# An attention and long-convolution kernel: the prologue's seed stages three slots sooner, first maxima over eight PSUM tiles, second unit's leading maxima ahead of the loop

## The chip, the cores and the metric

The kernel runs on one core of a Trainium2 chip. The time is that of one execution on the device, in microseconds (us); below it all durations come from one profiled execution. Engines are named as in the profile: PE (TensorE, matmuls; PEld its weight loads), DVE (VectorE), ACT (ScalarE), POOL (GpSimd), and SP (SyncE), which here issues the DMAs. Each engine executes its instructions in the order in which they stand, and an instruction that waits holds up what stands behind it on its engine.

## The reference

Two independent results are laid side by side in the output. Part A is a state-space convolution over 2048 positions and 448 channels; part B is softmax attention over 2048 positions with 16 heads of 28.

```python
def _A_ref(u, log_A_real, A_imag, C_real, C_imag, log_dt, D_skip):
    dt = jnp.exp(log_dt)
    A = -jnp.exp(log_A_real) + 1j * A_imag
    C = (C_real + 1j * C_imag) * dt[:, None]
    P = jnp.exp((A * dt[:, None])[:, :, None] * pos[None, None, :])
    K = 2.0 * jnp.einsum("dn,dnl->dl", C, P).real
    ...
    return y + u * D_skip[None, None, :]

def _B_ref(x, wqkv, wo):
    ...
    scores = jnp.einsum("bhqd,bhkd->bhqk", q, k) * scale
    p = _softmax(scores, axis=-1)
    o = jnp.einsum("bhqk,bhkd->bhqd", p, v)
    return (lambda x, *d: x.transpose(*d))(o, 0, 2, 1, 3).reshape(B, S, D) @ wo

a = _A_ref(A_u, A_log_A_real, A_A_imag, A_C_real, A_C_imag, A_log_dt, A_D_skip)
b = _B_ref(B_x, B_wqkv, B_wo)
return jnp.concatenate([a, b], axis=-1)
```

y is the causal convolution of u with K, done with FFTs. All data are float32; the kernel keeps precision by splitting operands in a high and a low part (xh and xl, hl).

## The kernel before, in words

**Two phases.** `body` has a prologue and a loop. The prologue projects x to q, k and v (part B) and computes the seeds of the powers of exp(A dt) (part A). It keeps both in DRAM. The loop runs 16 units (4 groups of 4 heads by 4 chunks of 512 queries) by 16 key tiles. In each step it computes scores (`s_mm`, tile pss), their exponentials on ACT (p), the products with v (`pv_step`, tile po), one part of the row maxima of the next unit (`max_mm`), and pieces of part A.

**The prologue's projections.** x comes in four chunks of 512 rows (`load_x`, tile xn). Each chunk is transposed on PE into pt tiles, split into xh and xl, and multiplied with the weights (wqkv, loaded into tri tiles, split by ACT and DVE into khat, vh and vl). There are 12 jobs a chunk, 48 in all: 8 of q or k and 4 of v, each 12 matmuls into one of three PSUM tiles pm (`w_tile`). ACT and DVE then evacuate it into hl (or xn in the last chunk) or vst, and SP writes it out. For k of the first two chunks, ACT and DVE form kb too, and POOL its low part dhl. The place of khat is that of the weights at first: head j of group 0 is loaded there (`load_k`) when both projections of group j in the last chunk are done.

**The seeds.** There are eight seeds (`seeds(o)`), each a list of stages: load the parameters (nat), exponentials and products with dt on ACT, transposes into a pn tile, phases and sizes, range reduction on DVE, sines on ACT, bases on POOL, complex products on DVE (px, pn, sg) and POOL (qhat, x_e), and two writes (sd). Parameters of the first one are loaded by `load_nat(0)`; dt is an exponential built from small DVE instructions on sg tiles (`exact_exp`), turned by PE in `turn_dt`.

**What sets the order.** Stages go into slots: stage i of seed o into slot 4 o + i, the loads two slots ahead of the seed (line 540). Before each slot's stages, as many projections are issued as PW = 37 slots need for 48 jobs. So there were 41 slots, the last four of them seeds alone. Within the prologue a scheduler then moves instructions on each engine; from `nc.kept = KEPT["a"]` (line 903) on, program order is kept. Each DMA carries one of eight completion names in rotation (DMAHW0 to DMAHW7), and waits for the earlier DMA that carried the same one.

**Unit 0's maxima** (lines 576 to 589). For each of 16 row blocks i, two pairs are reduced: kc 0 and 1 (`max_mm`, with kdif) and kc 2 and 3 (`max_pair`, with q_neg, the negated queries, so that PE forms a difference). Of each pair, ACT writes the Relu of the first tile into rl; DVE adds it to the second tile and takes the maximum (`tensor_tensor_reduce`, the CUSTOM_DVE_ANT rows). These use five PSUM tiles in turn, two pt and three pm, and two rl buffers. `max_join` and `max_end` turn the maxima (mh), and `max_put` writes them as two rows of unit 0's qhat, which the loop's first score matmul reads. Then the first LEAD = 3 blocks of unit 1's maxima follow, with four matmuls each.

Of the kernel before, what the change touches and what calls it, by code (L numbers as in the profile page):

```python
# [18 lines left out]
D = 448  # L19

H = 16
# [17 lines left out]
S0, SP, SW, SD, PW, E3 = 0, 4, 0, 5, 37, 8  # L39
# [51 lines left out]
def body(ctx, tc, a, out):  # L91
# [81 lines left out]
    def max_pair(i, kc, ps, q_neg):  # L173
        j, t = divmod(i, 4)
        ts = slice(t * 128, (t + 1) * 128)
        pm, kt = ps(), kt_g[0][j]
        if kc == 2:
            nc.tensor.matmul(pm, q_u[0][:, j, ts], kt[:, 2 * CQ:3 * CQ], start=True, stop=False)
            nc.tensor.matmul(pm, q_neg[:, j, ts], kt[:, 3 * CQ:], start=False, stop=True)
            rl_u[0, i] = kd_p.tile([128, CQ], F32, name="rl", bufs=2)  # L180
            nc.scalar.activation(rl_u[0, i], pm, AF.Relu)
        else:
            nc.tensor.matmul(pm, q_u[0][:, j, ts], kt[:, 3 * CQ:], start=True, stop=True)
            rl = rl_u.pop((0, i))
            nc.vector.tensor_tensor_reduce(rl, pm, rl, 1.0, -3.0e38, ALU.add, ALU.max, m_u[0][:, j, t, 1:2])
# [40 lines left out]
    with ExitStack() as st:  # L226
# [18 lines left out]
        load_x(0)  # L245
        w_g = k0_t[:CK].rearrange("p g (i s k h e) -> p i s k g h e", i=2, s=2, k=NCK, h=HG)
        vh = y_p.tile([CK, NCK, D], F32R, name="vh")
        vl = y_p.tile([CK, NCK, D], F32R, name="vl")
        nc.gpsimd.memset(k0_t[:CK].rearrange("p g (n e) -> p (g n) e", e=32)[:, :, DH:].bitcast(F32), 0.0)
        vst = [x_p.tile([128, H, 32], F32, name=f"vst{i}") for i in range(2)]  # L250
        for t in vst:
            nc.gpsimd.memset(t[:, :, DH:DH + 1], 1.0)
            nc.gpsimd.memset(t[:, :, DH + 1:], 0.0)
        wns = []
        for i in range(2):
            wn = t_p.tile([128, 3, LV, BO * 16], F32, name="tri", bufs=2).rearrange("p t k h -> p (t k h)")
            wn = wn[:CK, :2 * 3 * D].rearrange("p (k s d) -> p k s d", k=2, s=3)
            wns += [wn[:, 0], wn[:, 1]]
        for k in range(NCK):
            nc.sync.dma_start(wns[k], wqkv[k * CK:(k + 1) * CK, :].rearrange("p (s d) -> p s d", s=3))  # L260
        nc.sync.dma_start(kones, a["kones"])

# [3 lines left out]
        def load_nat(o):  # L266
            nats[o] = s_p.tile([PO, 4, 256], F32, name="nat", bufs=2)
            for i, n in enumerate(("A_log_A_real", "A_A_imag", "A_C_real", "A_C_imag")):
                nc.sync.dma_start(nats[o][:, i, :], bass.AP(tensor=a[n].tensor, offset=a[n].offset + first(o) * 256,
                                                            ap=[[256, JF // 4], [JF * 256, 4], [1, 256]]))  # L270
# [6 lines left out]
        for f in range(2):  # L277
            nc.sync.dma_start(ldt[4 * f:4 * f + 4, :].rearrange("o (j i) -> o j i", j=4), bass.AP(
                tensor=t.tensor, offset=t.offset + f * DF, ap=[[JF // 4, 4], [JF, 4], [1, JF // 4]]))
        load_nat(0)  # L280
        pw2 = s_p.tile([128, LV], F32, name="pw2")
        nc.sync.dma_start(pw2, a["pw2"])
        half_pi = s_p.tile([128, 1], F32, name="half_pi")
        nc.gpsimd.memset(half_pi, TWO_PI / 4)
        nc.sync.dma_start(sel, a["sel"])
        nc.sync.dma_start(w1, a["w1"])
        for k in range(NCK):
            for s in (1, 0):
                src = wns[k][:, s, :].rearrange("p (g h e) -> p g h e", g=G, e=DH)
                hi, lo = (w_g[:, i, s, k, :, :, :DH] for i in range(2))  # L290
                nc.scalar.activation(hi, src, AF.Copy)
                nc.vector.tensor_tensor(lo, src, hi.bitcast(F32), ALU.subtract)
            nc.scalar.activation(vh[:, k, :], wns[k][:, 2, :], AF.Copy)
            nc.gpsimd.tensor_tensor(vl[:, k, :], wns[k][:, 2, :], vh[:, k, :].bitcast(F32), ALU.subtract)
# [25 lines left out]
        def turn_dt():  # L320
            dt_ps = ps_t.tile([128, CQ], F32, name="pt")[:PO, :NO]
            nc.tensor.transpose(dt_ps, dt_o, ident[:NO, :NO])
            for i, f in enumerate((1.0, 0.15915494309189535, 2.0, -2.0, -1.0)):
                nc.vector.tensor_scalar(dt_all[:, i, :], dt_ps, f, None, op0=ALU.mult)

# [208 lines left out]
        n_stage = SP * (NO - 1) + len(stages[0])  # L534
# [3 lines left out]
        for o in range(NO):  # L538
            for i, st_ in enumerate(stages[o]):
                slots[max(SP * o + (i or -2), 0)] += st_  # L540
        slots[1].insert(0, turn_dt)
# [34 lines left out]
        more = [lambda: ps_t.tile([128, CQ], F32, name="pt")] * 2 + [w_tile] * 3  # L576
        n_st = ExitStack()
        q_neg = pool(n_st, "n_p").tile([128, HG, CQ], F32R, name="q_neg")
        for j in range(HG):
            nc.scalar.activation(q_neg[:, j], q_u[0][:, j].bitcast(F32), AF.Copy, scale=-1.0)  # L580
        for i in range(16):
            for kc in range(4):
                f, kw = (max_mm, (0, i, kc)) if kc < 2 else (max_pair, (i, kc))
                f(*kw, more[(4 * i + kc) % 5], *([q_neg] if kc > 1 else []))
        nc.scalar.activation(half_pi[:1], half_pi[:1], AF.Exp)
        n_st.close()
        max_join(0, 2)
        max_end(0, ps_t.tile([128, CQ], F32, name="pt"))
        max_put(0, nc.scalar)
# [314 lines left out]
    for b in range(3):  # L904
        load_sd(b, nc.sync if b else nc.scalar)
    for i in range(LEAD):
        for kc in range(4):
            max_mm(1, i, kc)
# [260 lines left out]
```

## Time and profile before

| what | value |
|---|---|
| median of 3 runs | 1283.33 us (1280.13 to 1284.64) |
| the profiled execution | 1284.67 us |
| its span, first to last instruction | 1282.8 us |
| mean granted PE clock | 0.981 |
| busy share of the span: PE, DVE, ACT, POOL | 95%, 72%, 75%, 66% |
| first score matmul of the loop | 234.41 us |

Line numbers hardly help in this profile: nearly every instruction passes through one helper (line 75), so rows are told apart by the names of the tiles that they write and read (out<-in). In a row of the timeline stand the start, the duration, the engine, the tiles and, in brackets, how long the engine had been idle and what released it. In a row of groups stand the busy time, the mean duration in ns and the idle time ahead. In the table by stretches each engine's busy time stands with its number of instructions, then the granted clock, the busy share of the DMA engines and the rate. The page's 40 slices show where the kernel is not full: PE dips in the sixth and seventh, that is from about 160 to 224 us.

```profile
PE   7988867999999999999999999999999999999987
POOL 2466651798778888877689999989995222324321
PEclk9988888899999999999999999999999999999999
```

### The profile page before, as it was taken

The numbers are of one execution on the slowest core, as the hardware profiler recorded it, in microseconds if no ns is written. First come the engines' busy times: TensorE is split into PE (matmuls) and PEld (weight loads), VectorE is DVE, ScalarE is ACT, GpSimd is POOL, SyncE is SP. The second block draws the span as 40 slices with busy tenths as digits, with TensorE's granted clock in tenths as the row PEclk, the third lists the DMA queues.
The fourth block names the chain that finished last, engine by engine and source line by source line (L and its number), as shares of the span: only waits on it lengthen the run. The fifth ranks groups of instructions, "written<-read, shape, count | busy, mean of one in ns | idle before, by whom it ended". The sixth has DMA issues, their size and how long they took to land.

```text
span 1282.8 us, 33335 instructions
## 1 busy us (share of the span) xinstructions
PE 1223.7 (95%) x12641; PEld 700.9 (55%) x12641; DVE 925.5 (72%) x2106; ACT 967.8 (75%) x2162; POOL 843.4 (66%) x728
## 2 busy tenths in 40 slices
PE   7988867999999999999999999999999999999987
PEld 5867754455555555555555555555555555544433
DVE  5788877787877787878778888888887645645111
ACT  4978856688888888888888888888887666656452
POOL 2466651798778888877689999989995222324321
PEclk9988888899999999999999999999999999999999
DMA  6767887446664544465533223432324533657665
GB/s 210 263 242 241 265 301 290 127 93 182 172 154 106 156 133 146 128 214 195 169 102 91 61 76 106 149 88 71 83 59 154 175 135 132 205 171 227 194 171 165
DMA packets 200089, 205.36 MB, mean 160 GB/s; under 512 B 95992, under 2 KB 158520, under 8 KB 197880
## 3 DMA queue, kind: packets, MB, share of 16 engines
q1 hardware_dynamic: 199720, 202.87, 51.4%
q8 instruction: 100, 1.64, 0.5%
q10 hardware_dynamic: 208, 0.36, 0.1%
q14 instruction: 61, 0.50, 0.1%
HBM read 120.73 MB, written 82.18 MB: 158 GB/s over the span
## 4 chain that ended last, share of the span: by engine, by line
PE 77%; DVE 7%; ACT 5%; POOL 5%; issue 3%; DMA 2%; SPq 0%; ACTq 0%; POOLq 0%; DVEq 0%
PE pm L75 44%; PE pss L75 16%; PE po L75 16%; POOL e L75 1%; ACT tri L75 1%; DVE mx L75 1%; ACT rl L75 1%; PE pt L75 1%; POOL qhat L75 1%; DVE sg L75 1%; DVE hl L75 1%; DVE tri L75 1%; POOL x_e L75 1%; DVE px L75 1%; POOL p L75 1%
## 5 line engine op out<-in xcount | busy, mean ns | idle before, releaser
L75 ACT ACTIVATE p<-pss 128x512 f32<-128x512 f32 x1024 | 561.4, 611 | 112.8 <-PE pss L75 108.5
L75 PE MATMUL pss<-qhat,khat 128*128 128x512 f32 x1024 | 402.7, 399 | 1.5 <-ACT p L75 1.4
L75 DVE TENSOR_REDUCE mx<-pm 128x1 f32<-128x512 f32 x480 | 308.6, 684 | 109.6 <-PE pm L75 107.5
L75 PE MATMUL pm<-khat,qhat 128*128 128x512 f32 x749 | 326.4, 439 | 5.3 <-ACT rl L75 3.0
L75 POOL TENSOR_TENSOR e<-e,sdb 128x256 f32<-128x256 f32 x168 | 201.9, 1202 | 108.1 <-ACT e L75 62.4
L75 PE MATMUL po<-p,v 128*32 128x512 f32 x2048 | 269.1, 594 | 0.0
L75 POOL TENSOR_TENSOR e<-e,eu 128x256 f32<-128x256 f32 x168 | 248.0, 1476 | 13.2
L75 PEld LDWEIGHTS pm<-khat,qhat 128*128 128x128 f32 x749 | 141.4, 189 | 201.3 <-ACT p L75 52.0
L75 DVE CUSTOM_DVE_ANT_0 rl<-pm,rl 128x512 f32<-128x512 f32 x259 | 178.4, 689 | 71.6 <-ACT rl L75 68.4
L75 PEld LDWEIGHTS pss<-qhat,khat 128*128 128x128 f32 x1024 | 190.4, 188 | 46.1 <-issue 10.8
L75 POOL TENSOR_TENSOR eu<-e,sdb 128x256 f32<-128x256 f32 x168 | 202.0, 1202 | 0.0
L75 POOL TENSOR_TENSOR p<-pr,pr 64x448 f32<-64x448 f32 x64 | 73.1, 1142 | 160.4 <-PE pm L75 135.2
L75 ACT ACTIVATE rl<-pm 128x512 f32<-128x512 f32 x259 | 157.1, 607 | 12.7 <-PE pm L75 7.9
L75 DVE TENSOR_TENSOR g<-g,zg 128x128 f32<-128x128 f32 x392 | 162.2, 414 | 3.4
L75 PE MATMUL pm<-kdif,qhat 128*128 128x512 f32 x249 | 101.1, 406 | 8.5 <-DVE xn L75 6.6
L75 PE MATMUL pm<-xh,khat 112*128 112x512 f32 x256 | 87.0, 422 | 9.2 <-DVE kb L75 4.4
L75 DVE TENSOR_TENSOR zg<-g,zg 128x128 f32<-128x128 f32 x224 | 87.9, 393 | 5.1
L75 PEld LDWEIGHTS pm<-e,g 128*32 128x32 f32 x3584 | 57.2, 109 | 43.8 <-issue 16.1
L75 DVE TENSOR_TENSOR pr<-pm,ub 128x448 f32<-128x448 f32 x64 | 37.0, 620 | 56.2 <-PE pm L75 41.8
L75 PE MATMUL pm<-e,g 128*32 128x64 f32 x3584 | 73.0, 222 | 1.9 <-POOL e L75 1.9
L75 ACT ACTIVATE y<-pm 128x448 f32<-128x448 f32 x48 | 26.5, 553 | 58.2 <-PE pm L75 34.1
L75 ACT ACTIVATE ub<-pm 128x224 f32<-128x224 f32 (+1 forms) x96 | 38.8, 450 | 39.9 <-PE pm L75 37.6
(134 smaller groups left out, 1465.5 us busy)
## 6 DMA issues: line engine op xcount, KB each, us to landing
sdb<-sd SPq DMA_DIRECT2D x55, 336.0 KB
qhat<-q SPq DMA_DIRECT2D x64, 256.0 KB
khat<-k SPq DMA_DIRECT2D x64, 256.0 KB
sd<-sg SPq DMA_DIRECT2D x8, 1456.0 KB
k<-hl SPq DMA_DIRECT2D x16, 512.0 KB
mw<-in_mw SPq DMA_DIRECT2D x16, 512.0 KB
sd<-qhat SPq DMA_DIRECT2D x8, 896.0 KB
yu_d<-ub SPq DMA_DIRECT2D x64, 112.0 KB
```

Source lines behind the costliest of these rows:

```text
L75: i = f(*args, **kw)
```

## The change

Five things are done.

1. `SH = 3` takes three slots off every stage; the load, too, from slot 4 o - 2 to 4 o - 5 (none below slot 0). The number of slots falls from 41 to 38 (the projections still use 37). `turn_dt` moves from slot 1 to slot 0.
2. The parameters come first: dt's loads, `load_nat(0)` and dt's exponential move ahead of the loads of x and the weights, and their six DMAs go on ACT's queue in place of SP's. kones is loaded after pw2.
3. Unit 0's maxima take eight PSUM tiles in turn (two pt, two pn, one px, three pm) in place of five, and in the order kc 0, 2, 1, 3. The rl of the second pair comes from a pool of its own with three buffers, so there are five in all.
4. The three leading blocks of unit 1 are computed in the prologue, over the same eight tiles, right behind `max_put`. Their PSUM tiles belong to the prologue's pools, whose places the loop's tiles take later.
5. `max_put(0)` and the first sd load go on SP's queue, where they had been on ACT's.

```diff
-S0, SP, SW, SD, PW, E3 = 0, 4, 0, 5, 37, 8
+SP, SH, PW, E3 = 4, 3, 37, 8
...
-    def max_pair(i, kc, ps, q_neg):
+    def max_pair(i, kc, ps, q_neg, rl_p):
...
-            rl_u[0, i] = kd_p.tile([128, CQ], F32, name="rl", bufs=2)
-            nc.scalar.activation(rl_u[0, i], pm, AF.Relu)
+            rl_u[0, i, 1] = rl_p.tile([128, CQ], F32, name="rl", bufs=3)
+            nc.scalar.activation(rl_u[0, i, 1], pm, AF.Relu)
...
+        def load_nat(o, queue=nc.sync):
+            nats[o] = s_p.tile([PO, 4, 256], F32, name="nat", bufs=2)
+            for i, n in enumerate(("A_log_A_real", "A_A_imag", "A_C_real", "A_C_imag")):
+                queue.dma_start(nats[o][:, i, :], bass.AP(tensor=a[n].tensor, offset=a[n].offset + first(o) * 256,
+                                                          ap=[[256, JF // 4], [JF * 256, 4], [1, 256]]))
...
+            nc.scalar.dma_start(ldt[4 * f:4 * f + 4, :].rearrange("o (j i) -> o j i", j=4), bass.AP(
+                tensor=t.tensor, offset=t.offset + f * DF, ap=[[JF // 4, 4], [JF, 4], [1, JF // 4]]))
+        load_nat(0, nc.scalar)
...
         load_x(0)
...
-        n_stage = SP * (NO - 1) + len(stages[0])
+        n_stage = SP * (NO - 1) + len(stages[0]) - SH
...
-                slots[max(SP * o + (i or -2), 0)] += st_
-        slots[1].insert(0, turn_dt)
+                slots[max(SP * o + (i - SH if i else -2 - SH), 0)] += st_
+        slots[0].insert(1, turn_dt)
...
-        more = [lambda: ps_t.tile([128, CQ], F32, name="pt")] * 2 + [w_tile] * 3
+        p_t, p_n, p_x = (lambda p=p, n=n: p.tile([128, CQ], F32, name=n) for p, n in ((ps_t, "pt"), (ps_n, "pn"), (ps_x, "px")))
+        more = [p_t, w_tile, p_t, w_tile, p_n, w_tile, p_n, p_x]
...
         for i in range(16):
-            for kc in range(4):
-                f, kw = (max_mm, (0, i, kc)) if kc < 2 else (max_pair, (i, kc))
-                f(*kw, more[(4 * i + kc) % 5], *([q_neg] if kc > 1 else []))
+            for n, kc in enumerate((0, 2, 1, 3)):
+                ps = more[(4 * i + n) % 8]
+                max_mm(0, i, kc, ps) if kc < 2 else max_pair(i, kc, ps, q_neg, n_p)
         nc.scalar.activation(half_pi[:1], half_pi[:1], AF.Exp)
-        n_st.close()
         max_join(0, 2)
-        max_end(0, ps_t.tile([128, CQ], F32, name="pt"))
-        max_put(0, nc.scalar)
+        max_end(0, p_t())
+        max_put(0, nc.sync)
+        for i in range(LEAD):
+            for kc in range(4):
+                max_mm(1, i, kc, more[(4 * i + kc + 1) % 8])
+        n_st.close()
         sst.close()
...
     for b in range(3):
-        load_sd(b, nc.sync if b else nc.scalar)
-    for i in range(LEAD):
-        for kc in range(4):
-            max_mm(1, i, kc)
+        load_sd(b)
```

The scheduler makes a new order of the whole prologue from this. Three places show it. The first is the start on SP, with the completion names that each DMA waits for. Before:

```order
L75 DMA ident<-in_ident 128x128
L75 DMA xn<-in_B_x 128x2x448 x2
L75 DMA tri<-in_B_wqkv 112x1344 x4
L75 DMA kones<-in_kones 128x1
L75 DMA sg<-in_A_log_dt 4x4x14 [waits DMAHW0_49]
L75 DMA sg<-in_A_log_dt 4x4x14 [waits DMAHW1_49]
L75 DMA nat<-in_A_log_A_real 56x1x256 [waits DMAHW2_49]
```

Now, on SP:

```order
L75 DMA ident<-in_ident 128x128
L75 DMA xn<-in_B_x 128x2x448 x2
L75 DMA tri<-in_B_wqkv 112x1344 [waits DMAHW1_49]
L75 DMA tri<-in_B_wqkv 112x1344 [waits DMAHW2_49]
L75 DMA tri<-in_B_wqkv 112x1344 [waits DMAHW3_49]
L75 DMA tri<-in_B_wqkv 112x1344 [waits DMAHW4_49]
```

and on ACT, at its very start, where no DMA stood before:

```order
L75 DMA sg<-in_A_log_dt 4x4x14 x2
L75 DMA nat<-in_A_log_A_real 56x1x256
L75 DMA nat<-in_A_A_imag 56x1x256
L75 DMA nat<-in_A_C_real 56x1x256
L75 DMA nat<-in_A_C_imag 56x1x256 [waits DMAHW0_49]
L75 ACT_TABLE_LOAD
L75 ACTIVATE nat<-nat 56x256 [waits DMAHW4_49]
L75 ACTIVATE xh<-pt 112x512 [waits PE_49] x2
```

Five of the parameters' six DMAs are now among the first eight, which need not wait for a name; the weight loads (tri) no longer are. And ACT's first xh stands behind six issues and the first exponential.

The second place is DVE where the last seed ends. `xn<-pm_..., xn` is the evacuation of the last projection; px, sg and qhat rows are seeds; rows with `rl,mx` are unit 0's maxima. Before:

```order
L75 TENSOR_TENSOR sg<-sg,px 128x2x7x16
L75 TENSOR_TENSOR xn<-pm_1939,xn 128x512
L75 TENSOR_TENSOR qhat<-qhat 128x7x16
L75 TENSOR_TENSOR px<-qhat 128x112
L75 TENSOR_TENSOR qhat<-qhat 128x7x16
L75 TENSOR_TENSOR qhat<-qhat,px 128x7x16
L75 TENSOR_TENSOR px<-qhat 128x112
L75 TENSOR_TENSOR qhat<-qhat,px 128x7x16
L75 TENSOR_TENSOR px<-pn,gz 128x224
L75 TENSOR_TENSOR sg<-pn,tri 128x2x7x16
L75 TENSOR_TENSOR px<-sg,px 128x224
```

Now:

```order
L75 TENSOR_TENSOR px<-pn,gz 128x224
L75 SCALAR_TENSOR_TENSOR hl<-pm_1954,kones,hl 128x512
L75 TENSOR_TENSOR sg<-sg,px 128x2x7x16
L75 TENSOR_TENSOR sg<-px,tri 128x2x7x16
L75 TENSOR_TENSOR px<-px,gz 128x224
L75 TENSOR_TENSOR sg<-sg,px 128x2x7x16
L75 TENSOR_TENSOR xn<-pm_1987,xn 128x512
L75 ISA rl,mx<-pt,rl 128x512
L75 ISA mx 128x1
L75 ISA rl,mx<-pn,rl 128x512
L75 ISA mx 128x1
```

Before, fourteen seed rows stood between the last evacuation and the first maximum; now none does, and the first maxima alternate between pt and pn tiles.

The third place is ACT between unit 0's last rl, the maxima's transfer (qhat<-mh) and unit 1's leading rl. Before:

```order
L75 ACTIVATE rl<-pm_2261 128x512
L75 ACTIVATE rl<-pt 128x512
L75 ACTIVATE rl<-pm_2276 128x512
L75 DMA qhat<-mh 1x16x128 x2
L75 DMA sdb<-sd_81 128x672
L75 ACTIVATE rl<-pm_2326 128x512
```

Now:

```order
L75 ACTIVATE rl<-pm_2258 128x512
L75 ACTIVATE rl<-pn 128x512
L75 ACTIVATE rl<-pm_2273 128x512
L75 ACTIVATE rl<-pm_2295 128x512
L75 ACTIVATE rl<-pm_2308 128x512
L75 ACTIVATE rl<-pm_2321 128x512
```

The three DMAs have left ACT; they stand on SP behind the last write of sd, with the sdb and ua loads behind them.

72 lines of the change are left out of this document (34 added, 38 removed).

## The prediction

> **What bounds the kernel now.** The profiled execution took 1284.67 us, 1282.8 of them the span; the median of the three runs is 1283.33, 1.34 below it. I read the busy time by stretches first, cut where the chain of waits changes: start-up; the projections with the seeds between them; the seeds' tail; unit 0's maxima; unit 1's leading maxima; the loop.
>
> ```profile
> core 0: us, PE busy (x) PEld busy (x) DVE busy (x) ACT busy (x) POOL busy (x), PEclk, DMA share, GB/s
> 0.00:20.00 20.00, 11.93 (x42) 9.13 (x43) 7.91 (x12) 9.26 (x17) 7.15 (x20) 1.00 0.72 204
> 20.00:143.00 123.00, 109.37 (x506) 87.76 (x504) 101.38 (x206) 100.48 (x247) 70.47 (x92) 0.94 0.74 252
> 143.00:180.20 37.20, 36.69 (x158) 30.08 (x158) 28.22 (x48) 30.73 (x74) 15.46 (x20) 0.92 0.76 253
> 180.20:195.40 15.20, 2.54 (x6) 1.34 (x5) 12.51 (x28) 3.48 (x14) 13.60 (x19) 0.60 1.02 359
> 195.40:224.90 29.50, 25.02 (x75) 14.52 (x75) 21.47 (x64) 20.42 (x37) 1.34 (x2) 0.86 0.75 276
> 224.90:234.40 9.50, 7.10 (x14) 3.64 (x15) 5.88 (x15) 2.30 (x5) 1.08 (x2) 0.64 0.65 208
> 234.40:1282.80 1048.40, 1031.03 (x11843) 554.38 (x11841) 748.14 (x1738) 801.11 (x1771) 734.32 (x577) 1.00 0.47 139
> ```
>
> The loop holds PE for 1031.03 of 1048.40 us and the change touches nothing in it, so I carry its 1048.4 us over whole. What can move is the 234.4 us ahead of it. There PE sits nearly empty in one stretch, 180.2 to 195.4 (2.54 us busy, clock 0.60), while DVE (12.51) and POOL (13.60) finish the last seeds. In the last quarter of the projections, 143 to 180.2, PE is full (36.69 of 37.2); in 20 to 143 no engine is full, DVE and ACT stand at 82%.
>
> The chain of waits, in order of time, shows how the hole and the two stages behind it hang together:
>
> ```profile
> 188.18 0.70 DVE xn L75
> 188.88 0.04 issue
> 188.93 0.50 PE pm L75
> 189.43 5.75 DMA khat<-k
> 195.18 0.39 ACT sg L75
> 195.58 0.43 ACT rl L75
> 196.00 2.07 ACT q_neg L75 x4
> ...
> 225.91 1.90 DMA qhat<-mh
> 227.83 0.61 ACT rl L75
> 228.48 6.10 PE pm L75 x10
> ```
>
> The last projection, whose matmuls ended at 180.2, has its low part formed by DVE only at 188.18, behind seed rows. The last eight khat loads and ACT's copies of the seeds (sg at 195.18) stand before the first rl. So the seeds set the start of unit 0's maxima, through the in-order queues of ACT, DVE and SP.
>
> **The hole (seeds three slots sooner).** The DVE order shows the effect: the last seed's rows now lie ahead of the last projection's evacuation, which the maxima follow at once. Of the 12.51 us of DVE in the hole two evacuations are no seeds (0.73 and about 0.67, rows below), so 11.1 us of DVE work must fit ahead of PE's end. In return the parameters' exponential goes to the start:
>
> ```profile
> L75 DVE TENSOR_TENSOR xl<-pt,xh 112x512 fp32r<-112x512 f32 x4 | 2.8, 692 | 9.6 <-ACT xh L75 9.6
> L75 DVE TENSOR_SCALAR sg<-sg 8x56 f32<-8x56 f32 x10 | 1.7, 174 | 0.2
> L75 DVE TENSOR_TENSOR sg<-sg 8x56 f32<-8x56 f32 x6 | 1.7, 276 | 0.1
> L75 DVE SCALAR_TENSOR_TENSOR hl<-pm,kones,hl 128x512 fp32r<-128x512 f32 x2 | 1.5, 732 | 0.0
> L75 DVE TENSOR_TENSOR hl<-pm,hl 128x512 fp32r<-128x512 f32 x1 | 0.7, 671 | 0.0
> L75 DVE SCALAR_TENSOR_TENSOR sg<-sg 8x56 f32<-8x56 f32 x3 | 0.6, 204 | 0.1
> L75 DVE COPY sg<-sg 8x56 f32<-8x56 f32 x1 | 0.2, 203 | 0.0
> L75 DVE CAST sg<-sg 8x56 int32<-8x56 f32 x1 | 0.2, 171 | 0.0
> ```
>
> These sg rows are 1.7 + 1.7 + 0.6 + 0.2 + 0.2 = 4.4 us, and the 9.6 us that DVE waits before the first xl rows hide them. Net 6.7 us of DVE work is added between 20 and 180.2, where DVE is free for 21.6 + 9.0 = 30.6 us. If that work ran at the 82% of the stretch 20 to 143, the projections would end 6.7 / 0.82 = 8.1 us later; if it all fell into waits, 0. Between the two I take 3: it lands in the first chunks, which no engine fills, and the last 37 us are held by PE anyway, where DVE has 9 us free. PE's end is then 183.2. Behind it stand ACT's evacuation (0.6), the first rl (0.6), and up to 0.5 of seed rows on DVE; the first maximum on DVE starts at about 185. Before, it started at 196.04 (row below). **Gain 11.0, bounds 3 and 14**: 14 if the projections end no later; 3 if they end 8.1 later and the first khat loads cost another 3, about half of the 5.75 above. POOL's 13.6 us moves too; POOL is 57% busy from 20 to 143, so I cost it at nothing beside the 3 us. If that cover fails, evacuations that wait for POOL hold PE; that is the slower rival.
>
> **Parameters first, on ACT's queue.** The order puts six issues ahead of ACT's first work, and SP's four weight loads now each wait for an earlier load; before they went out without a wait.
>
> ```profile
> 2.17 1.95 SPq L75 DMA_DIRECT2D tri<-in_B_wqkv  x4
> 4.63 1.60 SPq L75 DMA_DIRECT2D sg<-in_A_log_dt  x2
> 4.66 2.23 PE L75 MATMUL pt<-ident,xn 128*112 128x128 f32 x8 [4.66 <-DMA xn<-in_B_x]
> 6.28 1.02 SPq L75 DMA_DIRECT2D nat<-in_A_log_A_real  x1
> 9.53 1.04 ACT L75 ACTIVATE khat<-tri 112x448 fp32r<-112x448 f32 x2 [2.44 <-DMA tri<-in_B_wqkv]
> ```
>
> The first x load had landed at 4.66. If the first weight load waits for it, it goes out 2.5 us later than at 2.17; the end on the other side is 0, since DMA engines were 0.72 busy up to 20 us and the x loads come first anyway. ACT's six issues take 1.6 + 4 x 1.0 = 5.6 us by these rows, and ACT had no weights to work on before 9.53, which covers them. **Cost 1.0, bounds 0 and 2.5**, nearer to 0 because the queue is kept busy by x meanwhile. [...]
>
> **Unit 0's maxima over eight tiles.** 32 reductions run on DVE from 196.04 to 224.91, 28.9 us:
>
> ```profile
> L75 DVE CUSTOM_DVE_ANT_0 rl<-pm,rl 128x512 f32<-128x512 f32 x19 | 13.0, 690 | 5.8 <-ACT rl L75 4.4 <-PE pm L75 0.9
> L75 DVE CUSTOM_DVE_ANT_0 rl<-pt,rl 128x512 f32<-128x512 f32 x13 | 9.0, 690 | 2.7 <-ACT rl L75 2.3
> L75 ACT ACTIVATE rl<-pm 128x512 f32<-128x512 f32 x19 | 11.1, 596 | 4.5 <-PE pm L75 3.4 <-DVE mx L75 0.6 <-PE pt L75 0.3
> L75 ACT ACTIVATE q_neg<-qhat 128x512 fp32r<-128x512 f32 x4 | 2.2, 618 | 0.0
> ...
> 196.04 0.69 DVE L75 CUSTOM_DVE_ANT_0 rl<-pt,rl 128x512 f32<-128x512 f32 x1 [1.06 <-ACT rl L75]
> ```
>
> DVE's work stays (21.5 us). Its idle, 5.8 + 2.7 less the 1.06 ahead of the first, is 7.4, nearly all waiting for ACT's rl, which waited for PE, which waited for one of five tiles or two rl buffers. Now there are eight tiles and three more rl buffers for the folded half. ACT's q_neg, 2.2 us in one piece plus an rl of 0.6, still holds DVE once. That leaves about 2.9 us idle. **Gain 4.5, bounds 0 and 7.4.** PE has room: 25.02 us at a mean clock of 0.86, less if the clock is whole.
>
> **Unit 1's leading maxima ahead, one queue.** DVE stands still between the mh rows and the first leading rl, since ACT issues the mh transfers and one sdb load ahead of its rl:
>
> ```profile
> 225.86 0.28 DVE L75 SCALAR_TENSOR_TENSOR mh<-pt,mh 16x128 fp32r<-16x128 f32 x1
> 225.91 1.25 ACTq L75 DMA_DIRECT2D qhat<-mh  x2
> 228.46 0.69 DVE L75 CUSTOM_DVE_ANT_0 rl<-pm,rl 128x512 f32<-128x512 f32 x1 [2.32 <-ACT rl L75]
> 229.08 1.28 DVE L75 TENSOR_REDUCE mx<-pm 128x1 f32<-128x512 f32 x2
> 234.41 0.41 PE L75 MATMUL pss<-qhat,khat 128*128 128x512 f32 x1
> ```
>
> The 2.32 us go, as the transfers move to SP. There qhat<-mh stands behind the last sd write, and sdb and ua loads stand behind it. The mh transfer took 1.90 and the leading reductions take three times 0.69 + 1.28 = 5.9 us, so the transfer is hidden. The loop's score tiles lie where the eight tiles lay and must wait for DVE to read the last of those, which gives part of it back. **Gain 1.5, bounds 0 and 2.3.**
>
> Sum: 11.0 - 1.0 + 4.5 + 1.5 = 16.0. From 1284.67 that is 1268.7, and 1.34 less for the median: **1267 us**.
>
> **Rivals.** (a) The projections pay in full: DVE keeps its 82%, PE ends at 188.3, the hole yields 5.9; the sum is 10.9 and the time 1272. For it: no engine is full and yet PE loses 13.6 us from 20 to 143, so waits are set by in-order queues and not by load. Against: the 9.6 us at the start. (b) The khat loads hold the maxima: the DMA engines are 1.02 busy at 359 GB/s in the hole, and SP issues in order behind the q and k writes. If the load at the chain's 5.75 stays whole behind PE's end, the first maxima start 5 us later: sum 11, again 1272; against it, only the rows of heads 0 and 1 are needed first, and their place is released two projections sooner. (c) Both, with no gain from the tiles because the 690 ns reductions keep waiting for ACT: 16.0 - 5.1 - 5 - 4.5 = 1.4, so 1282. (d) Slower: PE starves in the projections. Seed rows now precede evacuations on ACT and DVE; three projection tiles wait for them, PE idles, and its clock falls as in the hole (0.60). With a mean clock of 0.80 in place of 0.94 over 20 to 143, 109.4 us of matmuls become 128.5, 19 more, and idle added to it 5: PE ends at 204, the first reduction starts at 206, the hole gives -10, the start -1; with 4.5 and 1.5 that is 5 us slower, 1288, and more where it starves longer. The sign turns at a PE end of 199. Against it: the clock held 0.94 at about the same seeds per chunk.
>
> **How the numbers follow.** Forecast 1267: 0.50. (a) 0.18, (b) 0.14, (c) 0.10, (d) 0.08. All bounds at their best give 14 + 7.4 + 2.3 = 23.7 and 1259.6; (c) is near their worst. The range 1258 to 1281 leaves out (d) and half of (c). About 0.3%, 3.85 us, is what a measurement tells from no change: faster means below 1279.5. The forecast, (a), (b) and a little of (c) are faster: 0.84; the rest of (c) and a mild (d) are the same: 0.09; slower 0.07.
>
> **What would show it.** After the change: PE's last projection matmul at about 183 with no stretch of 10 us below 30% busy behind it; the first reduction rl at about 185 (later than 190 speaks for (a) or (b): for (a) if PE's end is late too, for (b) if DVE then waits for a khat load); 32 reductions in about 24 us, idle once for q_neg; ACT's first khat row at about 10.5; less than 1 us of DVE idle between mh and the next rl; the first pss at about 218.4; 1048 us from there. A loop longer than 1050 us, or a PE end past 199, would make the prediction wrong.

## The result and the profile after

The changed kernel takes 1279.87 us (median of 20 runs, 1276.66 to 1282.5) against 1282.09 us of the kernel before (20 runs, 1280.07 to 1284.64): ratio 0.9985, 95% interval 0.9978 to 0.9992. That is 2.2 us less, where the prediction had 16.0 and a time of 1267. The time lies inside the predicted range, near its upper end, but the gain is within the 0.3% that was called no change. The ratio of the repetition (again, below) leaves out two slow executions, of 1364.71 and 4017.98 us.

The profiled execution of the changed kernel took 1278.54 us. The table by stretches, cut at its own stages: start, projections (two rows), from PE's last projection matmul to the first reduction, unit 0's reductions, unit 1's lead, loop.

```profile
core 0: us, PE busy (x) PEld busy (x) DVE busy (x) ACT busy (x) POOL busy (x), PEclk, DMA share, GB/s
0.00:20.00 20.00, 12.51 (x44) 9.13 (x45) 11.22 (x38) 11.05 (x22) 6.97 (x20) 1.00 0.89 239
20.00:143.00 123.00, 109.23 (x487) 86.80 (x486) 100.41 (x186) 100.28 (x252) 74.43 (x97) 0.90 0.70 242
143.00:186.80 43.80, 39.91 (x179) 31.92 (x178) 34.04 (x65) 31.11 (x76) 27.94 (x34) 0.96 0.80 257
186.80:190.80 4.00, 1.54 (x5) 0.98 (x5) 1.46 (x3) 1.97 (x5) 1.72 (x2) 0.90 0.96 360
190.80:220.00 29.20, 24.55 (x76) 16.55 (x75) 20.79 (x64) 18.81 (x34) 0.00 (x0) 0.78 0.97 347
220.00:228.20 8.20, 5.41 (x15) 3.94 (x16) 6.35 (x15) 2.41 (x5) 0.92 (x2) 0.75 1.04 355
228.20:1276.70 1048.50, 1031.75 (x11843) 555.22 (x11841) 748.02 (x1737) 801.42 (x1771) 734.59 (x577) 1.00 0.48 138
```

The hole of 15.2 us behind the projections has shrunk to 4.0, as the change means it to. But the projections end at 186.8, not at 183: between 20 and 143 us PE issued 487 matmuls where it had issued 506, at almost the same busy time, so its clock was lower (0.90 against 0.94). The first reduction starts at 190.8 (predicted 185), because PE now waits for khat:

```profile
189.74 0.51 PE L75 MATMUL pm<-khat,qhat 128*128 128x512 f32 x1 [2.46 <-DMA khat<-k]
190.05 0.63 PE L75 MATMUL pt<-khat,qhat 128*128 128x512 f32 x1
...
193.45 0.39 PE L75 MATMUL pn<-khat,qhat 128*128 128x512 f32 x1
...
196.19 0.48 PE L75 MATMUL pt<-khat,qhat 128*128 128x512 f32 x1 [1.39 <-DMA khat<-k]
```

The matmuls of 0.63 us right behind the first wait ran at a granted clock of 0.50 (190.03 to 193.44); at 193.45, with the clock at 1.00 again, one of the same shape takes 0.39. The reductions take 29.2 us (28.9 before; predicted about 24), and the first pss comes at 228.2 (predicted 218.4). The loop takes 1048.5 us in this profile, as before; in the second profile of the change (again, below) it takes 1053.5. The two profiles differ by 6.2 us at the first pss, the medians by 2.2: how much of that was the one execution is told by repetitions below.

### The profile page after: what moved, and what is told of

Same layout as the page of the kernel before. It is cut to its first block, busy times and chain, and to the rows that moved or that the text cites. A ratio compares the mean times of both kernels' runs of the same rounds, so it can differ in the third digit from the quotient of the medians.

```text
span 1276.7 us, 33336 instructions
## 1 busy us (share of the span) xinstructions
PE 1224.9 (96%) x12641; PEld 704.5 (55%) x12641; DVE 922.3 (72%) x2106; ACT 967.1 (76%) x2162; POOL 846.6 (66%) x728
## 4 chain that ended last, share of the span: by engine, by line
PE 75%; DVE 7%; DMA 5%; ACT 4%; POOL 4%; issue 3%; SPq 1%; ACTq 0%; POOLq 0%; DVEq 0%
PE pm L75 42%; PE pss L75 16%; PE po L75 16%; POOL e L75 1%; DVE mx L75 1%; DMA k<-hl 1%; ACT tri L75 1%; DVE tri L75 1%; DMA v<-vst 1%; SPq L75 1%; DMA khat<-k 1%; POOL qhat L75 1%; DVE rl L75 1%; POOL p L75 1%; DVE hl L75 1%
## 5 line engine op out<-in xcount | busy, mean ns | idle before, releaser
L75 PE MATMUL pm<-khat,qhat 128*128 128x512 f32 x737 | 321.3, 437 | 5.4 <-DMA khat<-k 2.5
L75 DVE CUSTOM_DVE_ANT_0 rl<-pm,rl 128x512 f32<-128x512 f32 x245 | 168.8, 689 | 67.7 <-ACT rl L75 61.6
L75 PE MATMUL pm<-kdif,qhat 128*128 128x512 f32 x240 | 96.1, 400 | 3.2 <-DVE mx L75 2.4
```

What stands on the lines that cost most here:

```text
L75: i = f(*args, **kw)
```

## The experiments

All ratios are against the kernel before, run beside it on the same chip. The milestones come from one profile each, in us, and single profiles of one kernel differ by up to 4 us at the first pss (before and before_again): PE's last projection matmul; DVE's last seed row; the first reduction; the time from there to the end of the 32nd; the first pss.

| kernel | ratio (95% interval) | PE's end | seeds' end | first rl | 32 rl | first pss |
|---|---|---|---|---|---|---|
| before, the first profile | 1 | 180.2 | 195.0 | 196.0 | 28.9 | 234.4 |
| before_again | 0.9997 (0.9988 to 1.0006) | 177.1 | 191.9 | 192.9 | 28.3 | 230.5 |
| the change | 0.9985 (0.9978 to 0.9992) | 186.8 | 187.6 | 190.8 | 29.2 | 228.2 |
| again (the change) | 0.9982 (0.9970 to 0.9995) | 187.5 | 188.3 | 191.3 | 27.7 | 228.0 |
| u_seeds | 0.9951 (0.9939 to 0.9963) | 176.6 | 187.2 | 188.3 | 26.6 | 223.0 |
| u_tiles | 0.9969 (0.9958 to 0.9981) | 186.4 | 187.2 | 190.1 | 27.1 | 227.6 |
| u_lead | 0.9986 (0.9974 to 0.9998) | 186.4 | 187.2 | 188.9 | 26.8 | 227.1 |
| u_params | 1.0005 (0.9993 to 1.0018) | 193.7 | 193.7 | 195.4 | 26.3 | 231.6 |
| p_only | 0.9954 (0.9942 to 0.9966) | 177.9 | 188.5 | 189.6 | 27.2 | 226.3 |
| s_only | 1.0004 (0.9994 to 1.0015) | 193.2 | 193.2 | 195.9 | 27.0 | 233.8 |
| p_lead | 0.9937 (0.9923 to 0.9950) | 178.1 | 188.1 | 189.2 | 27.1 | 225.1 |
| sh1 | 0.9922 (0.9903 to 0.9940) | 179.6 | 183.7 | 185.3 | 25.9 | 220.0 |
| sh1_five | 0.9928 (0.9914 to 0.9943) | 177.1 | 181.2 | 184.3 | 27.2 | 220.1 |
| sh1_qpool | 0.9909 (0.9894 to 0.9925) | 178.0 | 182.1 | 183.8 | 25.3 | 218.2 |
| sh2 | 0.9886 (0.9869 to 0.9902) | 177.1 | 178.5 | 180.1 | 25.6 | 215.0 |
| sh2_again | 0.9893 (0.9878 to 0.9908) | 176.6 | 177.9 | 179.6 | 26.1 | 213.8 |
| sh2_five | 0.9913 (0.9901 to 0.9926) | 182.5 | 183.3 | 186.5 | 26.8 | 222.1 |
| sh2_qpool | 0.9915 (0.9894 to 0.9936) | 176.7 | 177.9 | 179.6 | 25.6 | 214.4 |
| early3 | 0.9966 (0.9953 to 0.9979) | 182.7 | 185.0 | 186.7 | 28.2 | 223.1 |
| late3 | 0.9951 (0.9936 to 0.9967) | 186.3 | 186.2 | 187.9 | 25.5 | 221.5 |

### One part undone at a time

**u_seeds**, the stages back at their old slots:

```diff
-SP, SH, PW, E3 = 4, 3, 37, 8
+SP, SH, PW, E3 = 4, 0, 37, 8
...
-        slots[0].insert(1, turn_dt)
+        slots[1].insert(0, turn_dt)
```

> The changed kernel with the seed stages back at their old slots; the other three parts stay. Theory A (the moved seed work comes back almost in full ahead of PE's end, and the maxima then run into the khat loads and the low clock): with the seeds late again the khat loads have landed when the maxima start, so the eight tiles can work and the 32 reductions take 24 to 26 us instead of the 29.1 of the changed kernel; first reduction at 196, first pss 226 to 228, time within 1.5 us of the changed kernel's 1279.9. Rival B (the whole gain comes from the seeds, the tiles are worth nothing anywhere): reductions again in 28.5 to 29.5 us from 196, time 1282 to 1285, no faster than the kernel before.

Measured 0.9951: the kernel without the seeds' move is faster than the change by 4.4 us (0.9951 against 0.9985, of 1282), more than either theory had, and both had the first reduction at 196. The first reduction starts at 188.3 without any slot moved, and PE's projections end 10.2 us sooner than in the change.

**u_tiles**, the five old tiles and the old order of parts:

```diff
-        more = [p_t, w_tile, p_t, w_tile, p_n, w_tile, p_n, p_x]
+        more = [p_t, p_t, w_tile, w_tile, w_tile]
...
-            for n, kc in enumerate((0, 2, 1, 3)):
-                ps = more[(4 * i + n) % 8]
+            for n, kc in enumerate((0, 1, 2, 3)):
+                ps = more[(4 * i + n) % 5]
...
-                max_mm(1, i, kc, more[(4 * i + kc + 1) % 8])
+                max_mm(1, i, kc)
```

> The changed kernel with unit 0's maxima over the five old tiles in the old order of parts, and unit 1's lead over the old tiles. Theory A (in the changed kernel khat loads, the q_neg copies and PE's granted clock pace the maxima, not the tiles): the reductions take 29 to 31 us as before, time within 1.5 us of 1279.9. Rival (the tiles are worth the predicted 4.5 us and something else ate it): reductions in 33 us, time about 1284.

Measured 0.9969, 27.1 us of reductions: the rival, 4.5 us lost without the eight tiles, falls, and so do the 29 to 31 us of theory A. The edit takes back the eight tiles and their order, but not the three more rl buffers; that holds for all runs here with five tiles but the kernel before and s_only. Whether five are even better here stays open; the intervals touch.

**u_lead**, unit 1's lead and the queues as before:

```diff
-        max_put(0, nc.sync)
-        for i in range(LEAD):
-            for kc in range(4):
-                max_mm(1, i, kc, more[(4 * i + kc + 1) % 8])
+        max_put(0, nc.scalar)
...
     for b in range(3):
-        load_sd(b)
+        load_sd(b, nc.sync if b else nc.scalar)
+    for i in range(LEAD):
+        for kc in range(4):
+            max_mm(1, i, kc)
```

> The changed kernel with unit 1's leading maxima back behind the start of the kept order, and the mh copies and the first seed load on ACT's queue. If this part is worth what its gap says (mean gap from mh to the first leading reduction 2.3 before, 0.7 after), the time is 1.5 us above the changed kernel: about 1281.4. Rival: the gap is refilled by the wait for sdb that follows on ACT, and the time is within 0.5 us of 1279.9.

Measured 0.9986, no difference that the interval shows; a gain of 1.5 us lies within it.

**u_params**, the parameters back behind the weights:

```diff
-        load_nat(0, nc.scalar)
...
-        exact_exp(dt8, ldt, [NO, PO])
...
         load_x(0)
...
+        load_nat(0)
...
+        exact_exp(dt8, ldt, [NO, PO])
```

> The changed kernel with the seeds' parameters loaded and exponentiated at their old place, behind the weights and on SP's queue; seed stages three slots sooner. If the parameters first cost nothing and are needed for the sooner seeds: first seed rows 3 to 10 us later, PE's projection end 1 to 4 us later than 186.8, time 1280 to 1284. Rival (loading them first pushed the weights back, as the prediction charged with 1.0): time 1278 to 1279, the first khat row on ACT 1 us earlier.

Measured 1.0005: the whole gain is gone. PE's end moves by 7 us to 193.7, far beyond the 4 expected. The part that had been booked as a cost carries the gain.

### One part alone, and other numbers of slots

**p_only** (the kernel before with the parameters first), **s_only** (before with `SH = 3`) and **p_lead** (before with the parameters first and the lead ahead) are made of the same edits; p_only and p_lead also keep the three more rl buffers of the change, which the kernel before and s_only lack.

> The kernel before with the parameters first and nothing else of the change. Theory P (the seeds end sooner because their first exponential starts sooner, and that, not the slots, is what brings the first reduction forward): seeds' last row on DVE at 187 (195.0 before), PE's projection end 176 to 177, first reduction at 188, ratio 0.993 to 0.996. Rival S (the slots bring it; the parameters only cost DVE time at the start): seeds end at 195, ratio 0.999 to 1.002.

> The kernel before with the seed stages three slots sooner and nothing else of the change. Theory P (the slots only change which of the two, projections or seeds, ends last; the work of DVE, ACT and POOL ahead of the maxima stays): seeds' end stays near 194, PE's projection end moves to 193 or 194, khat loads go out behind it, ratio 1.001 to 1.005. Rival S (the slots fill the hole): PE's end by 184, first reduction by 187, ratio 0.991 to 0.994.

> The kernel before with the parameters first and unit 1's leading maxima ahead on one queue; five tiles, old slots. Against the run without the seeds' move (ratio 0.9951) it lacks only the eight tiles. If the tiles are worth something where the khat loads are early: first to last reduction 28 to 29 us instead of 26.6, ratio 0.996 to 0.998. Rival (the tiles are worth nothing anywhere, as the run without them under the moved seeds suggests): 0.994 to 0.9955.

Measured 0.9954, 1.0004 and 0.9937. Theory P holds: the parameters alone bring 5.9 us (0.0046 of 1282), and the slots alone bring nothing, with PE's end at 193.2, as that theory had it. p_lead came out better than either expectation, so here too eight tiles show no worth in the time. The extra rl buffers are no likely cause of p_only's gain: s_only has two and takes 27.0 us for the reductions, p_only has five and takes 27.2. What the parameters move stands in three DVE rows, the start of the exponential, its turned form (dt_all) and the first of a seed's phases, in the kernel before and then in p_only:

```profile
21.06 0.60 DVE L75 TENSOR_SCALAR sg<-sg 8x56 f32<-8x56 f32 x3
28.33 0.45 DVE L75 TENSOR_SCALAR dt_all<-pt 56x8 f32<-56x8 f32 x5 [0.35 <-PE pt L75]
33.36 0.28 DVE L75 TENSOR_SCALAR tri<-pn 128x112 f32<-128x112 f32 x1 [1.18 <-PE pn L75]
```

```profile
2.97 0.69 DVE L75 TENSOR_SCALAR sg<-sg 8x56 f32<-8x56 f32 x3 [2.97 <-DMA sg<-in_A_log_dt]
16.80 0.30 DVE L75 TENSOR_SCALAR dt_all<-pt 56x8 f32<-56x8 f32 x3 [2.08 <-PE pt L75]
24.59 0.26 DVE L75 TENSOR_SCALAR tri<-pn 128x112 f32<-128x112 f32 x1
```

The first seed starts 8.8 us sooner, and the last one ends 3.3 us sooner than in the second profile of the kernel before, 6.4 than in the first. Two readings are left: the seeds follow their sooner start, or DVE has 4.4 us of small instructions less in its busy stretch. The last seed's end moves by about the 4.4 us and not by 8.8; no run separates the two.

**sh1**, one slot:

```diff
-SP, SH, PW, E3 = 4, 3, 37, 8
+SP, SH, PW, E3 = 4, 1, 37, 8
```

> The changed kernel with the seed stages one slot sooner instead of three. If every slot sooner delays PE's projection end by about 3.4 us (10.2 over three) and the first reduction waits for the later of seeds' end and khat loads: PE's end near 180, first reduction at 188, ratio 0.995 to 0.997. Rival (one slot is free, the third one does the harm, and the better balance gains): ratio 0.993 to 0.9945.

Measured 0.9922, better than either expectation: PE's end is where it was expected, but the first reduction starts 3 us sooner than expected, at 185.3. PE's end alone would still fit 3.4 us a slot (176.6 without a move); sh1_five, sh1_qpool and sh2 below, with PE's ends of 177.1, 178.0 and 177.1, do not, so the rule falls.

**sh2** (`SH = 2`), **sh1_five** (one slot, five tiles), **sh1_qpool** (one slot, and the edit below) and **again** (the change itself):

```diff
-            nc.scalar.activation(q_neg[:, j], q_u[0][:, j].bitcast(F32), AF.Copy, scale=-1.0)
+            nc.gpsimd.tensor_scalar(q_neg[:, j], q_u[0][:, j].bitcast(F32), -1.0, None, op0=ALU.mult)
```

> The changed kernel with the seed stages two slots sooner instead of three. If PE's projection end and the seeds' end cross between one slot (179.6 and 183.7) and three (186.8 and 187.6), and the later of the two sets the first reduction: PE's end 182 to 184, first reduction 186 to 188, ratio 0.993 to 0.996. Rival (one slot was a lucky fit and nothing is monotonic): as slow as three slots, 0.998 to 1.000.

> One slot sooner (ratio 0.9922), but unit 0's maxima over the five old tiles. If eight tiles are worth what the phases of the runs so far say (27.0 to 27.2 us with five, 25.9 to 26.8 with eight): 0.5 to 1 us, ratio 0.9925 to 0.993. Rival (the predicted 4.5 us where nothing else is in the way): 0.9955 to 0.996.

> One slot sooner, with q_neg formed on POOL, which has no work there, instead of ACT, where it stands behind the first relus and DVE idles 1.86 us for it. If that wait is on the path: the phase of reductions 1 to 1.9 us shorter, ratio 0.9907 to 0.9915. Rival (khat loads of the next heads then hold the reductions in its place): ratio 0.9920 to 0.9925.

> The changed kernel itself, for a second profile. If the 29.18 us of its reductions in the first profile were the granted clock of that execution (0.78 in the phase) and not the code: 26 to 28 us now, ratio 0.998 to 0.999. Rival (the phase is 29 us by its code): 29 us again.

sh2 measured 0.9886, beyond both expectations: a first reduction at 180.1, with PE's end no later than without any move. sh1_five measured 0.9928 and sh1_qpool 0.9909, each close to its first expectation in the ratio, though the intervals overlap that of sh1; the reductions of sh1_qpool are 0.6 us shorter than sh1's, not 1 to 1.9. again shows 27.7 us of reductions in place of 29.2, with a granted clock over them of 0.89 in place of 0.78, so the first number was partly that execution's.

### Where the third slot hurts, and two repetitions

**early3** and **late3** set the shift by seed. Shown is late3; in early3 the expression is the other way round, and the number of slots in all is that of `SH = 2`. **sh2_five** and **sh2_qpool** are sh2 with the edits shown above.

```diff
         for o in range(NO):
             for i, st_ in enumerate(stages[o]):
-                slots[max(SP * o + (i - SH if i else -2 - SH), 0)] += st_
+                sh = 2 if o < 3 else 3
+                slots[max(SP * o + (i - sh if i else -2 - sh), 0)] += st_
```

> Two slots sooner, but three for the first three of the eight seed stages. Theory E (the changed kernel loses its 9.7 us of projection end in the stretch 60 to 100 us, where it is 32 matmuls behind the version with two slots; the stalls there belong to the early stages' interleaving with the second chunk): PE's projection end 184 to 187, ratio 0.995 to 0.998. Rival L (the last stages, which end in the same slot as the projections, do the harm): PE's end 177 to 179, ratio 0.988 to 0.990.

> Three slots sooner, but two for the first three of the eight seed stages: the counterpart. Theory E: PE's projection end 177 to 180, ratio 0.987 to 0.991. Rival L: PE's end 184 to 187, ratio 0.995 to 0.998.

> Two slots sooner, with q_neg formed on POOL instead of ACT. If the 1.3 thousandths that this brought at one slot (0.9922 to 0.9909) hold: ratio 0.987 to 0.988, the fastest version. Rival (the khat loads, closer behind now, hold the reductions instead, or POOL's q_neg of 1.49 us each comes too late): 0.9885 to 0.990.

> Two slots sooner, unit 0's maxima over the five old tiles. If eight tiles are worth 0.5 to 1.5 us, as the phases say (25.6 us with eight here, 27.2 with five at one slot): ratio 0.989 to 0.990. Rival (worth nothing in the time, as at no slot and at three): 0.987 to 0.9888.

> The version with two slots again, since its two relatives in the last runs came out at 0.9913 and 0.9915. If 0.9886 was no lucky set of executions: ratio 0.987 to 0.9905, first reduction at 180 to 182. Rival (PE's end of 177.1 was a lucky one of a spread that reaches 182.5 with the same order of instructions): ratio 0.990 to 0.992.

> The kernel before itself, for a second profile. The profile that the prediction read took 1284.67 us, 2.6 above the median of 20. If that was the granted clock of that execution (0.87 over the reductions, 28.9 us): reductions in 27 to 27.5 us as in the other runs with five tiles, first pss at 232 to 233. Rival (the profile was typical): 28.9 us and 234.4 again.

early3 measured 0.9966, late3 0.9951, with PE's ends of 182.7 and 186.3. Neither theory holds: each expects one of the two to be harmless, and both are slower than sh2. early3's PE end is no later than that of sh2_five, 182.5; its harm shows in the ratio and in PE's waits (below). sh2_qpool gains nothing over sh2. DVE's waits over its reductions say why; sh2 first, then sh2_qpool:

```profile
DVE rl L75 <- ACT rl L75: 2.3, 3, 1.9
DVE rl L75 <- PE pt L75: 1.6, 1, 1.6
```

```profile
DVE rl L75 <- PE pt L75: 2.2, 2, 1.9
DVE rl L75 <- ACT rl L75: 1.6, 3, 1.0
```

The columns are the total, the number of waits and the longest. The longest wait for ACT, behind q_neg, falls from 1.9 to 1.0, and the wait for PE grows. sh2_five measured 0.9913, 3.0 us above the mean of sh2's two ratios; yet 5.4 of the 7.1 us by which its first pss is later are PE's later projection end, up to which its instructions stand in the same order as sh2's. sh2_again confirms the best version: 0.9893. before_again shows the kernel before 4 us further ahead at the first pss than the profile that the prediction read, with PE's end at 177.1; its 28.3 us of reductions lie between the two expectations.

**Why PE ends later with three slots.** The same stretches of the change and then of sh2:

```profile
20.00:60.00 40.00, 34.88 (x165) 27.55 (x163) 29.05 (x53) 32.38 (x81) 20.27 (x29) 0.92 0.64 219
60.00:80.00 20.00, 17.86 (x71) 13.72 (x72) 15.37 (x29) 14.62 (x36) 12.05 (x14) 0.82 0.65 218
80.00:100.00 20.00, 17.50 (x69) 14.27 (x68) 17.55 (x31) 16.37 (x43) 13.88 (x17) 0.83 0.68 246
100.00:180.00 80.00, 72.11 (x334) 57.70 (x333) 66.58 (x124) 66.14 (x165) 51.84 (x67) 0.96 0.78 259
```

```profile
20.00:60.00 40.00, 34.10 (x164) 27.75 (x164) 31.77 (x56) 33.79 (x84) 20.29 (x29) 0.91 0.72 244
60.00:80.00 20.00, 19.36 (x88) 15.11 (x87) 17.00 (x32) 17.32 (x43) 13.65 (x18) 1.00 0.69 234
80.00:100.00 20.00, 16.79 (x81) 13.98 (x79) 17.39 (x34) 15.84 (x43) 13.92 (x17) 0.92 0.85 296
100.00:180.00 80.00, 72.55 (x336) 58.41 (x335) 70.57 (x134) 65.15 (x164) 57.45 (x68) 0.98 0.84 279
```

Between 60 and 100 us the change issues 140 matmuls, sh2 169. PE's busy time differs by 0.8 us, its clock by about 0.13 on average. Over the whole stretch from 20 us to PE's end, PE is busy for 149.15 us in the change and 141.4 in sh2, with nearly the same work (664 and 661 matmuls), and idle for 17.65 and 15.72. Of the 9.7 us between these two profiles, 7.75 are busy time, most of it slower matmuls: an estimate from the mean granted clock of each 5 us, with 0.50 (the change's clock from 53.5 to 67.1) as the low value, gives about 27.2 us at half in the change and 13.6 in sh2. 1.9 are waits. A row of waits precedes the slow part in the change:

```profile
54.78 1.10 PE L75 MATMUL pn<-ident,nat 56*128 56x56 f32 x8 [2.73 <-ACT nat L75]
55.81 1.22 PE L75 MATMUL pm<-xh,khat 112*128 112x512 f32 x2
56.83 0.63 PE L75 MATMUL pm<-xl,khat 112*128 112x512 f32 x1
57.25 1.91 PE L75 MATMUL pm<-xh,khat 112*128 112x512 f32 x4
60.84 1.10 PE L75 MATMUL pt<-ident,xn 128*112 128x128 f32 x4 [1.68 <-DVE xl L75]
61.59 0.78 PE L75 MATMUL pm<-xl,khat 112*128 112x512 f32 x1
```

The granted clock is 0.50 from 53.5, in the first of these waits, to 67.1 (rows in the last section). sh2 has a longer wait there, 4.17 us for ACT's nat at 53.92, and its clock is 0.73 on average from 50 to 55, 0.59 from 55 to 60 and 1.00 from 60 to 95: by the same estimate half for about 6.8 us only.

The waits alone do not set PE's end. The stretch from 20 us to it, in u_seeds, sh1, sh2, sh2_five, the change, early3 and late3:

```profile
20.00:176.56 156.56, 145.12 (x661) 117.03 (x660) 127.64 (x233) 129.72 (x320) 89.71 (x115) 0.93 0.76 259
20.00:179.55 159.55, 145.38 (x665) 117.77 (x664) 131.76 (x243) 130.99 (x324) 100.93 (x126) 0.95 0.76 257
20.00:177.12 157.12, 141.40 (x661) 114.73 (x661) 134.98 (x249) 130.60 (x325) 103.13 (x129) 0.96 0.79 265
20.00:182.47 162.47, 146.78 (x669) 118.85 (x667) 135.73 (x252) 132.92 (x330) 104.94 (x130) 0.94 0.77 260
20.00:186.80 166.80, 149.15 (x664) 118.72 (x663) 134.45 (x250) 131.39 (x326) 102.37 (x130) 0.92 0.73 246
20.00:182.72 162.72, 144.05 (x668) 115.44 (x667) 131.65 (x247) 129.83 (x323) 97.02 (x128) 0.96 0.76 253
20.00:186.25 166.25, 146.49 (x664) 117.77 (x663) 134.62 (x251) 131.73 (x326) 102.08 (x131) 0.93 0.76 257
```

PE is idle for 11.4, 14.2, 15.7, 15.7, 17.7, 18.7 and 19.8 us (the stretch less PE's busy time). Over all profiles that keep the parameters first it is 11.4 to 14.8 without a move, 14.1 to 14.6 with one slot, 15.6 to 15.8 with two and 17.4 to 19.3 with three. So each slot adds waits, but with one and two slots PE's end stays at 176.6 to 179.6, apart from sh2_five's 182.5; only with three is it 186.4 to 187.5, in each of four profiles. In the change the waits and the slower matmuls come together.

By what ended the waits, the change waits longer than sh2 for DVE's hl (6.1 us against 1.3) and ACT's vst (2.5 against 0.2), and less for ACT's nat (3.0 against 5.7) and xh (0.7 against 3.8). Why this interleaving of seeds and evacuations makes them, in each half of the seeds, was not isolated.

## Why the prediction was wrong, step by step

- **The loop, carried over: right in the first profile.** 1048.5 us against 1048.4. In the second profile of the change it is 1053.5, past the 1050 that was to make the prediction wrong; why was not shown. Over all profiles the loop takes 1047.0 to 1053.5. Its start is no longer the same, either: from the first pss to the 21st it takes 16.0 and 16.1 us in the kernel before, 16.9 and 17.5 in the change and 17.8 and 18.1 in sh2, so 1 to 2 us of what is gained ahead of the first pss is lost behind it.
- **Where the forecast missed.** The first pss came at 228.2 in place of 218.4. The first reduction is 5.8 us later than forecast (190.8 in place of 185), of which 1.0 had been booked for the parameters, and the reductions take 4.8 us longer (29.2 in place of 24.4). That is rival (c), both kinds of delay and no gain from the tiles, with smaller delays than it had and with reductions that wait for PE (5.2 us) more than for ACT (3.0).
- **"Between the two I take 3": the step that failed.** It priced the later end of the projections, with bounds 0 and 8.1, because the seeds' DVE work "lands in the first chunks, which no engine fills". With three slots PE ended at 186.4 to 187.5 in four profiles that keep the parameters first: 6.6 us later than in the profile read for the prediction, 9.7 later than in the second one. Against the profiles with the parameters first and no slot moved (176.6 to 178.1) it is 8 to 11 us, past the upper bound. The bounds counted DVE's free time. What they leave out are PE's waits for evacuations in the in-order queues, and its clock, which falls to half around some of them (0.50 from 53.5 to 67.1 in the change): 17.4 to 19.3 us of waits and a clock of 0.92 to 0.93 up to PE's end with three slots, 15.6 to 15.8 and 0.94 to 0.96 with two. That is the mechanism of rival (d), with a milder clock than its 0.80 (0.90 from 20 to 143 us) and a PE end near that of (a) (188.3). Two slots did not move PE's end, so free DVE time did not decide it. A small slip adds to the step: of the two evacuations that were taken out of DVE's 12.51 us, one had run ahead of the stretch (179.50 to 180.24), so 11.8 us of seeds moved, not 11.1.
- **"the first maximum on DVE starts at about 185": rival (b), at half its price.** Behind PE's end stand 4.0 us in place of 1.7, because khat head 0 lands 2.46 us after PE has stopped. In the kernel before the hole had covered these loads: PE did its first khat matmuls at 189.52 without a wait for a DMA. The 5.75 us of khat loads in the chain, from which the bound was made, did not hold the first rl there; ACT's sg ahead of it waited 1.50 us for DVE's sg.
- **The gain of the hole was put down to the wrong part.** Of the 5.2 us by which the first reduction came sooner in the two first profiles (196.0 to 190.8), three slots bring none: without them it starts at 188.3. The parameters first bring it.
- **"Parameters first: cost 1.0": the size is not resolved, and it is only half of the step.** ACT's first khat row stands at 10.04 (forecast 10.5), against 9.53 and 8.94 in the two profiles of the kernel before. But s_only and u_params, with the parameters behind the weights, have 9.84 and 10.44, and the sixteen profiles with the parameters first have 9.33 to 10.88. On the other side p_only is 5.9 us faster, with its first seed 8.8 us sooner. The prediction gave this part no gain of its own: it took the exponential only as 4.4 us of DVE work that hides elsewhere, inside the hole's price. That all eight seeds hang on it as the head of their chain is the other reading, and not shown apart from the first.
- **Eight tiles, 4.5: mis-sized.** Phases with five tiles and the parameters or the slots moved take 26.8 to 27.2 us, the kernel before 28.3 and 28.9; with eight (and q_neg on ACT) they take 25.5 to 26.8 in seven profiles and 27.7 to 29.2 in three, the change's two among them. That is about 1 us at best, and in the time, at none, one, two and three slots, the effect has either sign (-0.0014, +0.0006, +0.0024, -0.0015 in the ratio), so it is not resolved. The 24.4 us assumed that only q_neg would still hold DVE, 2.9 us in all. In sh2 DVE also waits 1.6 us for PE, which waits 1.26 us for a khat load; in the change itself DVE stands idle for 8.3 us over the reductions (7.4 before). Its rows for pm and pt, in which 1.47 of the wait for PE lies ahead of the first reduction:

```profile
L75 DVE CUSTOM_DVE_ANT_0 rl<-pm,rl 128x512 f32<-128x512 f32 x8 | 5.5, 690 | 4.2 <-PE pm L75 2.4 <-ACT rl L75 1.9
L75 DVE CUSTOM_DVE_ANT_0 rl<-pt,rl 128x512 f32<-128x512 f32 x8 | 5.5, 689 | 4.4 <-PE pt L75 3.7 <-ACT rl L75 0.7
```

- **Unit 1's lead, 1.5: not resolved.** From the last reduction to the first pss the change takes 8.2 us in one profile and 9.1 in the other, the kernel before 9.5 and 9.3. DVE's idle time ahead of the first leading rl is 0.63 and 1.67, where it was 2.32 and 2.33. p_only and p_lead, which differ in this part alone, have 9.5 and 8.7; their ratios overlap.
- **The start of the sum was high.** The profile of 1284.67 us is 2.6 above the later median of 1282.09. The prediction took off 1.34, by the three runs then known.
- **The time of 1267 is reached, but by two slots.** sh2 takes 1267.35 us. PE's end does not move, the first reduction starts at 180, and DVE needs 25.6 us for the reductions: more gain from the hole than predicted, less from the tiles. That the sum comes out equal is luck.

## What to carry to other kernels

Work that is moved under a busy matmul stream is to be priced by the waits that it puts ahead of PE and by what PE's clock does around them, not by the free time of the engine that does it: two slots left PE's end where it was, and a third cost 12 us of the time, with 17.7 us of waits and a clock of 0.92 up to PE's end in the change, 15.7 and 0.96 in sh2. When a change has several parts, each is to be tried alone; here six small loads and some 20 tiny instructions, booked as a cost, were worth 5.9 us alone, and without them the rest of the change brought nothing. And a distance that can be set by one number is worth a sweep before it is explained.

## What the runs showed of the hardware

Cut where PE's granted clock changes, the change's stretch from 53.5 to 94.5 us reads 0.50 and 1.00 in turn:

```profile
53.50:67.10 13.60, 10.64 (x32) 8.17 (x33) 10.33 (x22) 9.45 (x29) 9.41 (x16) 0.50 0.88 287
67.10:80.80 13.70, 12.40 (x60) 9.31 (x60) 8.77 (x16) 10.36 (x20) 7.26 (x11) 1.00 0.60 212
80.80:84.20 3.40, 3.40 (x9) 2.37 (x9) 3.20 (x8) 1.88 (x6) 2.47 (x4) 0.50 1.03 370
84.20:94.50 10.30, 7.89 (x35) 6.28 (x34) 10.30 (x19) 8.21 (x27) 7.35 (x6) 1.00 0.59 213
```

The low stretch at 80.8 has PE busy for all of its 3.40 us. Ahead of it lie two short waits, of 0.86 and 0.27 us:

```profile
78.19 0.73 PE L75 MATMUL pm<-xh,khat 112*128 112x512 f32 x2 [0.86 <-DVE kb L75]
...
79.65 0.70 PE L75 MATMUL pn<-ident,nat 56*128 56x56 f32 x8 [0.27 <-ACT nat L75]
```

One order of instructions took different times: sh2 and sh2_five, the same up to the last projection, ended it at 177.1 and 182.5, and two profiles of the kernel before at 180.2 and 177.1. In sh2 and sh2_five one place can be compared directly:

```profile
137.00:157.70 20.70, 16.38 (x83) 12.96 (x83) 17.80 (x36) 16.68 (x42) 16.25 (x17) 1.00 0.79 254
139.30:160.00 20.70, 16.36 (x71) 12.89 (x70) 15.91 (x33) 15.95 (x41) 14.43 (x16) 0.84 0.77 251
```

PE has the same waits in both, 0.99, 1.26, 0.50 and 1.34 us in sh2 and 0.98, 1.29, 0.49 and 1.35 in sh2_five. Yet sh2's clock stays at 1.00, and sh2_five's is 0.59 on average from 150 to 155 and 0.73 from 155 to 160, by estimate half for about 6.8 us from 150.9, around the last of them; 3.0 of the 5.4 us by which sh2_five's projections end later arise behind it. So nearly the same waits stand beside two different clocks; what sets them apart was not shown.
